# Plain passes with w2 loaded whole, factors in DRAM layout and stores moved later; first pair's w1 factors made two at a time

## The chip, the core and the metric

The kernel runs on one core of a Trainium2 chip. The metric is the device time of one execution in microseconds. A program's engines each work through their own queue in order: TensorE (PE, with its weight loads as PEld), VectorE (DVE), ScalarE (ACT), GpSimd (POOL), and SyncE (SP), which here issues all transfers.

## The reference

```python
def _attn_ref(q, k, v):                       # (8, 8, 576, 64), chunks of 64 tokens
    scores = scale * np.matmul(q_c, k_c.transpose(0, 1, 2, 4, 3))
    scores = scores - np.max(scores, axis=-1, keepdims=True)
    attn = np.exp(scores)
    attn = attn / (np.sum(attn, axis=-1, keepdims=True) + 1e-09)
    return np.matmul(attn, v_c).reshape(B, H, S, D)

def _moe_ref(x, domain_probs, w1, w2):        # x (4608, 512), 4 experts, w1 (4, 512, 1024)
    p = domain_probs / (domain_probs.sum(-1, keepdims=True) + 1e-09)
    for e in range(E):
        h = np.maximum(x @ w1[e], 0.0)
        out += p[:, e:e + 1] * (h @ w2[e])
```

Attention within chunks of 64 tokens gives x; four dense experts follow, weighted by normalized probabilities. All is in float32.

## The kernel before, in words

The 4608 tokens are 9 blocks of 512. An expert's 1024 hidden columns are two halves, so a block goes through 8 passes. Block 0 is done by the *plain passes* n = 0 to 7; the other eight blocks are four pairs, and each pair takes 8 *later passes* (8 to 39). Each float32 operand is split in a high part (fp32r, by ACT) and a low part (the rest, a subtraction), and a product is three matmuls: hi·hi, hi·lo, lo·hi.

A plain pass has eight *steps*: four hidden blocks (12 matmuls of 512 columns each, `plain_hidden`, then `relu_parts`, L614 on ACT and L615 on DVE) and four output tiles (`Tile.whole`, 12 matmuls, `Tile.out` L905 on DVE). `plain_pass` hangs work beside the steps with `add(at, i, ...)`: what is added at step i is issued behind step i on every queue. The attention of the first pair (`Beside`) is spread over the steps, ahead of each step.

A later pass uses Strassen-Winograd products: 2x2 quads of the weights and tokens, seven products instead of eight. It needs the quads' four sums s1 to s4, the *factors*, made in hi and lo parts. The first 14 products of a pass are hidden (g1..g7, h1..h7, `LaterGroup`), the 14 of the pass before are outputs (a1..a7, b1..b7, `Outer`), woven in the order of `WOVEN`; a product is 6 matmuls. The first later pass, n = 8, has the 14 hidden products alone (`FIRST`, with the last plain tile held until after its second product). The weights come as *ring units*: seven DRAM slots per pass and side (`slots`), each with two (quad or sum, group) units, loaded into three wf tiles a side (`ring_load`, `RINGS`). A unit's tile comes free when both its products are done (`ring_next`).

So the plain passes also have to make and store the factors that all later passes load:

- w2: `w_loads(1, ...)` loads four raw quads into wraw at step 6 of the pass before; `w2_split` (steps 0 and 1) makes hi and lo for the plain pass itself; `Factors` makes the sums on DVE (L389, steps 1 and 2), their parts on ACT and POOL (L343, L346) and stores them (`keep`, L411; `keep_quad`, L420) at steps 2 to 6.
- w1: passes 8 to 14 make their own, in the first pair's passes: `half_load` and `HalfFactors` load a group's columns into scratch and sum them on POOL (L444), `ring_make` makes a unit (two instructions on ACT, L488, and two on POOL, L489), uses it as ring unit and stores it (L490). `make_next` takes one from the list `making` after every product. The w1 factors of pass 7 (slots of pass 15) are made in plain passes 2 to 5 (`LAST_W1`).
- In the last plain pass `half_load`, sums and makes for pass 8 run beside the steps, then at step 6 `first_load(1)` and `probs_load`, which brings the probabilities of pass 8 that `Scaled.hidden` (L771, DVE) multiplies with.
- `Scaled.hi` and `lo` (L783 ACT, L786 POOL) split the hidden blocks of later passes; `Outer.add` (L831, L833) sums the outputs.

Of the kernel before, what the change touches and what calls it, by code (L numbers as in the profile page):

```python
# [15 lines left out]
P = 128  # L16
# [15 lines left out]
def chunk_attention_moe(ctx: ExitStack, tc: tile.TileContext, qk, v, v0, dp, w1, w2, out):  # L32
# [290 lines left out]
    def w_load(i, n, f, k):  # L323

        if i == 0 and n:
            t = opool.tile([P, 2, 2 * P], F32, name=f"acc{NK + 2 * f + k}")
        else:
            t = wpool.tile([P, 2, 2 * P], F32, name="wraw", bufs=N_RAW)
        raw[i, f, k] = t
        e, half = divmod(n % n_pass, 2)  # L330
        rows, cols = slice(2 * k, 2 * k + 2), slice(f * 2 * P, (f + 1) * 2 * P)
        nc.sync.dma_start(out=t, in_=(w1, w2)[i][e, half, :, rows, cols])

    QUADS = ((0, 0), (0, 1), (1, 0), (1, 1))

    PAIR_QUADS = ((0, 0), (1, 1), (0, 1), (1, 0))

    def w_loads(i, n, order=QUADS):
        for f, k in order:
            w_load(i, n, f, k)  # L340
# [29 lines left out]
    def w2_quad(f, k):  # L370
        return [t[:, :, f * 2 * P : (f + 1) * 2 * P] for t in w2t[k]]

    def w2_split(f, k, eng=None):
        if f == 0:
            w2t[k] = [hpool.tile([P, 2, SUB], F32R, name=f"hf{part}{4 + k}") for part in ("h", "l")]
        split(eng or nc.gpsimd, raw[1, f, k], w2_quad(f, k))

    class Factors:


        def __init__(self, i, n, quads, ws, tags):
            self.i, self.n, self.made = i, n, {}
            self.ws, self.tags = ws, dict(zip(("s1", "s2", "s3", "s4"), tags))
            for f in range(2):
                for k in range(2):
                    setattr(self, f"a{f + 1}{k + 1}", quads[f, k])

        def less(self, name, a, b, out, eng, op=ALU.subtract):
            (eng or nc.gpsimd).tensor_tensor(out=out, in0=getattr(self, a), in1=getattr(self, b), op=op)  # L389
            setattr(self, name, out)  # L390

        def sum1(self, eng=None):
            self.less("s1", "a21", "a22", self.ws[:, 0], eng, ALU.add)

        def sum2(self, eng=None):
            self.less("s2", "s1", "a11", self.ws[:, 1], eng)

        def sum3(self, eng=None):
            self.less("s3", "a11", "a21", self.a21, eng)

        def sum4(self, eng=None):
            self.less("s4", "a12", "s2", self.a12, eng)

        def make(self, name, eng=None):
            pool, tag = self.tags[name]
            t = self.made[name] = pool.tile([P, 2, *UNIT[1:]], F32R, name=tag)
            split(eng or nc.gpsimd, by_group(getattr(self, name)), parts_of(t))
# [7 lines left out]
    def keep_quad(n, f, k):  # L415

        for g in range(2):
            to = slot(n, 1, f"a{f + 1}{k + 1}", g)
            for part, t in enumerate(w2_quad(f, k)):
                nc.sync.dma_start(out=to[:, part], in_=t[:, :, g * P : (g + 1) * P].bitcast(F32))  # L420
# [7 lines left out]
    class HalfFactors:  # L428


        AT = {"a11": 0, "a12": 1, "a21": 2, "a22": 3, "s1": 4, "s2": 5, "s4": 6, "s3": 2}

        def __init__(self, n, g, places):
            self.n, self.g = n, g
            self.at = {name: places[i // 2][:, i % 2] for name, i in self.AT.items()}
            e, half = divmod(n % n_pass, 2)
            for f in range(2):
                cols = slice((2 * f + g) * P, (2 * f + g + 1) * P)
                nc.sync.dma_start(
                    out=places[f].rearrange("p a b c -> p (a b) c"), in_=w1[e, half, :, :, cols]  # L440
                )

        def less(self, name, a, b, eng, op=ALU.subtract):
            (eng or nc.gpsimd).tensor_tensor(  # L444
                out=self.at[name], in0=self.at[a], in1=self.at[b], op=op
            )

        def sum1(self, eng=None):
            self.less("s1", "a21", "a22", eng, ALU.add)

        def sum2(self, eng=None):
            self.less("s2", "s1", "a11", eng)

        def sum3(self, eng=None):
            self.less("s3", "a11", "a21", eng)

        def sum4(self, eng=None):
            self.less("s4", "a12", "s2", eng)

    halves = {}  # L460
    scratch = []

    def half_load(n, g):
        if (n, g) == (n_pass, 0):
            places = [opool.tile([P, 2, 2, P], F32, name=f"acc{NK + i}") for i in range(4)]
        else:
            if not scratch:
                scratch.append(xpool.tile([P, NK * PAIR * SUB], F32, name="xraw"))
            at = SUB + g * 7 * 2 * P
            places = [  # L470
                scratch[0][:, at + i * 4 * P : at + min(i * 4 + 4, 14) * P].rearrange(
                    "p (a b c) -> p a b c", b=2, c=P
                )
                for i in range(4)
            ]
        halves[n, g] = HalfFactors(n, g, places)
# [3 lines left out]
    n_made = (n_pass - 1) * N_SLOT  # L480
    making = []

    def ring_make(r):
        t, (n, k) = ring[0, r], divmod(r, N_SLOT)
        for u in range(2):
            g, at = divmod(2 * k + u, 7)
            src = halves[n_pass + n, g].at[ORDER[0][at]]
            nc.scalar.copy(out=t[:, u, 0], in_=src)  # L488
            nc.gpsimd.tensor_tensor(out=t[:, u, 1], in0=src, in1=t[:, u, 0].bitcast(F32), op=ALU.subtract)  # L489
        nc.sync.dma_start(out=slots[n, 0, k], in_=t.bitcast(F32))  # L490

    def make_next():
        if making:
            making.pop(0)()

    def ring_load(i, r, tag=None):

        def begin():
            ring[i, r] = wpool.tile(
                [P, 2, *UNIT[1:]], F32R, name=f"wf{RINGS[i][r % 3] if tag is None else tag}"  # L500
            )
            if i == 0 and r < n_made:
                ring_make(r)
            else:
                nc.sync.dma_start(
                    out=ring[i, r].bitcast(F32), in_=slots[r // N_SLOT % n_pass, i, r % N_SLOT]
                )

        if i == 0 and r < n_made:
            making.append(begin)  # L510
        else:
            begin()
# [110 lines left out]
    def h_alloc(s, f):  # L623
        i, k = divmod(f, 2)
        if k == 0:
            hs[s, i] = [hpool.tile([P, 2, SUB], F32R, name=f"hf{part}{2 * s + i}") for part in ("h", "l")]
        return h_part(s, f)
# [100 lines left out]
    class Scaled:  # L728
# [25 lines left out]
        def part(self, name, i):  # L754
            if (name, i) not in self.parts:
                self.parts[name, i] = hpool.tile(
                    [P, 2, SUB], F32R, name=f"hf{'hl'[i]}{self.J[name]}"
                )
            return self.parts[name, i]
# [106 lines left out]
    class Tile:  # L866
# [7 lines left out]
        def part(self, fs, cols, first, last):  # L874
# [3 lines left out]
            if self.n == 0:  # L878
# [3 lines left out]
                self.ps, parts,  # L882
                lambda f, a: h_part(self.s, f)[a][:, self.i * P : (self.i + 1) * P],
                lambda f, b: w2t[f // 2][b][:, f % 2, cols],
# [170 lines left out]
    def load_all():  # L1055
# [4 lines left out]
        w_load(0, 0, 0, 0)  # L1060
        w_load(0, 0, 1, 0)
        start_load(2, slice(0, 2))
        w_load(0, 0, 0, 1)
        w_load(0, 0, 1, 1)
        start_load(3, slice(0, 2))
        w_load(1, 0, 0, 0)
        w_load(1, 0, 1, 0)
# [7 lines left out]
    def startup(beside):  # L1075
# [36 lines left out]
        w_load(1, 0, 0, 1)  # L1112
        w_load(1, 0, 1, 1)
# [8 lines left out]
        w2_split(1, 1)  # L1122
        less_max(sc[3])
# [20 lines left out]
        w_loads(0, 1)  # L1144
        for f in range(NK):
            plain_hidden(f, [2, 3], alloc=False, name=("B1", "B0", "A0", "C0")[f])
        w2 = w2_factors(0)
        w2.sum1()
        w2.sum2()
        w2.sum3()  # L1150
        w2.sum4()
        for i, (f, k) in enumerate(QUADS):
            w1_split(f, k, (nc.gpsimd, nc.vector)[i % 2])
        for name in ("s1", "s2", "s3", "s4"):
            w2.make(name)
        for quad in KEPT:
            keep_quad(0, *quad)
        for name in ("s1", "s2", "s3", "s4"):
            w2.keep(name)
        w_loads(1, 1, PAIR_QUADS)  # L1160
# [3 lines left out]
    KEPT = ((0, 0), (0, 1), (1, 1))  # L1164

    def w2_factors(n):
        quads = {quad: raw[1, *quad] for quad in QUADS}
        ws = wpool.tile([P, 2, 2, 2 * P], F32, name="ws")
        return Factors(1, n, quads, ws, [(hpool, name) for name in ("hfh6", "hfl6", "hfh3", "hfl3")])
# [36 lines left out]
    def plain_pass(n, beside, x):  # L1206
# [5 lines left out]
        for i in range(NK):  # L1212
            add(at, i // 2, lambda i=i: w2_split(*QUADS[i]))
            if not last_pass:
                add(at, i // 2, lambda i=i: w_load(0, n + 1, *QUADS[i]))
# [3 lines left out]
        w2 = []  # L1219
        add(at, 1, lambda: w2.append(w2_factors(n)), lambda: w2[0].sum1(nc.vector), lambda: w2[0].sum2(nc.vector))  # L1220
# [396 lines left out]
```

## Time and profile before

| | us |
|---|---|
| runs of the kernel | 1532.82, 1533.34, 1535.16 (median 1533.34) |
| profiled execution | 1533.17 |
| its span, first to last instruction | 1531.4 |
| PE, DVE, POOL, ACT busy | 1477.7, 1052.6, 997.1, 630.4 |
| mean granted TensorE clock | 0.989 of full |

A row of the windows view gives a stretch's length, each engine's busy time with its instruction count, the granted clock, the share of the 16 DMA engines and GB/s. A row of the waits view reads: who waited, its line, for whom, then total us, times, longest. A row of the lines view: line, engine, operation, written tile <- read tiles, shape, count | busy us, mean ns of one | idle us before them and what ended it. A row of the timeline: start, us, engine, line, operation, tiles, count, and in brackets the idle time before it. A matmul's shown duration is longer than the distance between two starts, since matmuls overlap.

### The profile page before, as it was taken

The numbers are of one execution on the slowest core, as the hardware profiler recorded it, in microseconds if no ns is written. First come the engines' busy times: TensorE is split into PE (matmuls) and PEld (weight loads), VectorE is DVE, ScalarE is ACT, GpSimd is POOL, SyncE is SP. The second block draws the span as 40 slices with busy tenths as digits, with TensorE's granted clock in tenths as the row PEclk, the third lists the DMA queues.
The fourth block names the chain that finished last, engine by engine and source line by source line (L and its number), as shares of the span: only waits on it lengthen the run. The fifth ranks groups of instructions, "written<-read, shape, count | busy, mean of one in ns | idle before, by whom it ended". The sixth has DMA issues, their size and how long they took to land.

```text
span 1531.4 us, 23579 instructions
## 1 busy us (share of the span) xinstructions
PE 1477.7 (96%) x8556; PEld 1207.4 (79%) x8556; DVE 1052.6 (69%) x1455; ACT 630.4 (41%) x1214; POOL 997.1 (65%) x818
## 2 busy tenths in 40 slices
PE   8899977899999999999999999999999999999998
PEld 7677755677777888888888888888888888888887
DVE  5556583566767788677777886777777966666665
ACT  3456542454545443434343344334343433333332
POOL 4667677999998776555555765555557655555554
PEclk9999988999999999999999999999999999999999
DMA  7799868576767777966666579666665596565655
GB/s 222 229 294 298 296 213 269 185 263 225 251 226 247 241 244 211 269 218 215 232 207 200 201 212 268 227 213 230 203 205 195 200 234 229 195 208 194 206 193 152
DMA packets 233236, 345.13 MB, mean 225 GB/s; under 512 B 71568, under 2 KB 151200, under 8 KB 233120
## 3 DMA queue, kind: packets, MB, share of 16 engines
q1 hardware_dynamic: 233120, 343.62, 69.4%
q8 instruction: 68, 1.11, 0.3%
q14 instruction: 48, 0.39, 0.1%
HBM read 273.23 MB, written 70.33 MB: 224 GB/s over the span
## 4 chain that ended last, share of the span: by engine, by line
PE 79%; POOL 8%; DMA 4%; DVE 3%; issue 3%; ACT 2%; SPq 2%; POOLq 0%; ACTq 0%; DVEq 0%
PE A L607 43%; PE C L607 23%; PE B L607 10%; POOL hfl L786 2%; POOL wf L489 1%; DMA wraw<-in_w 1%; PE psa L208 1%; POOL xraw L444 1%; POOL hfl L346 1%; PE psa L161 1%; SPq L411 1%; POOL hfh L346 1%; DMA w<-hfh 1%; POOL wf L346 1%; DMA acc<-in_w 1%
## 5 line engine op out<-in xcount | busy, mean ns | idle before, releaser
L786 POOL TENSOR_TENSOR hfl<-wraw,hfh 128x512 fp32r<-128x512 f32 x384 | 500.7, 1319 | 229.9 <-ACT hfh L783 227.2
L607 PE MATMUL A<-xh,wf 128*128 128x512 f32 (+1 forms) x1104 | 382.1, 389 | 0.0
L607 PE MATMUL A<-hfh,wf 128*128 128x512 f32 (+1 forms) x1024 | 358.2, 391 | 0.6 <-ACT acc L831 0.6
L783 ACT CAST hfh<-wraw 128x512 fp32r<-128x512 f32 x384 | 234.2, 622 | 285.0 <-DVE wraw L777 88.8
L607 PEld LDWEIGHTS A<-xh,wf 128*128 128x128 f32 x1104 | 207.7, 189 | 43.3
L669 ACT COPY s<-A 128x512 f32<-128x512 f32 x192 | 112.8, 587 | 290.6 <-PE A L607 290.4
L607 PEld LDWEIGHTS A<-hfh,wf 128*128 128x128 f32 x1024 | 192.1, 188 | 42.9 <-DVE acc L833 1.8
L607 PE MATMUL C<-xh,wf 128*128 128x512 f32 (+1 forms) x600 | 205.9, 390 | 11.1 <-DVE acc L905 10.4
L607 PE MATMUL A<-xl,wf 128*128 128x512 f32 (+1 forms) x552 | 214.4, 389 | 0.0
L833 DVE TENSOR_TENSOR acc<-A,acc 128x512 f32<-128x512 f32 x232 | 158.0, 681 | 78.5 <-PE A L607 77.6
L607 PE MATMUL A<-hfl,wf 128*128 128x512 f32 x512 | 199.0, 389 | 0.0
L607 PE MATMUL C<-hfh,wf 128*128 128x512 f32 x512 | 178.3, 389 | 0.0
L607 PEld LDWEIGHTS C<-xh,wf 128*128 128x128 f32 x600 | 111.9, 189 | 35.1 <-DVE acc L905 10.8
L777 POOL TENSOR_TENSOR wf<-wraw,wf 128x512 f32<-128x512 f32 x31 | 40.0, 1292 | 150.3 <-DVE wf L771 150.3
L833 DVE TENSOR_TENSOR acc<-C,acc 128x512 f32<-128x512 f32 x120 | 82.7, 689 | 68.3 <-PE C L607 58.9
L607 PE MATMUL B<-xh,wf 128*128 128x512 f32 (+1 forms) x376 | 125.3, 385 | 0.0
L607 PEld LDWEIGHTS A<-xl,wf 128*128 128x128 f32 x552 | 103.9, 189 | 21.4
L786 POOL TENSOR_TENSOR hfl<-wf,hfh 128x512 fp32r<-128x512 f32 x64 | 92.8, 1451 | 40.8 <-ACT hfh L783 40.4
L607 PE MATMUL C<-xl,wf 128*128 128x512 f32 (+1 forms) x300 | 115.1, 387 | 0.0
L607 PEld LDWEIGHTS C<-hfh,wf 128*128 128x128 f32 x512 | 96.1, 188 | 19.8
L607 PEld LDWEIGHTS A<-hfl,wf 128*128 128x128 f32 x512 | 96.1, 188 | 19.5
L607 PE MATMUL C<-hfl,wf 128*128 128x512 f32 x256 | 100.2, 391 | 6.8 <-POOL hfl L786 6.8
(200 smaller groups left out, 2401.9 us busy)
## 6 DMA issues: line engine op xcount, KB each, us to landing
wf<-w SPq DMA_DIRECT2D x399, 512.0 KB, 4.2
w<-wf SPq DMA_DIRECT2D x49, 512.0 KB, 3.0
qk_in<-in_qk SPq DMA_DIRECT2D x32, 512.0 KB, 4.9
wraw<-in_w SPq DMA_DIRECT2D x36, 256.0 KB, 5.1
w<-hfh SPq DMA_DIRECT2D x32, 256.0 KB, 3.2
w<-hfl SPq DMA_DIRECT2D x32, 256.0 KB, 4.0
acc<-in_w SPq DMA_DIRECT2D x30, 256.0 KB, 5.7
xraw<-in_w SPq DMA_DIRECT2D x26, 256.0 KB, 5.0
```

The lines of the kernel that those rows point to most:

```text
L161: nc.tensor.matmul(s["sc"][of_half(half), c, slot], lhsT=q, rhs=k, start=True, stop=True)
L208: nc.tensor.matmul(av[of_half(slot % 2), half, head // 2], lhsT=s["v"][of_half(half), head], rhs=s["pt"][of_half(half), c, slot], start=Tr ...
L346: eng.tensor_tensor(out=t[1], in0=src, in1=t[0].bitcast(F32), op=ALU.subtract)
L411: nc.sync.dma_start(out=slot(self.n, self.i, name, g), in_=self.made[name][:, g].bitcast(F32))
L444: (eng or nc.gpsimd).tensor_tensor(out=self.at[name], in0=self.at[a], in1=self.at[b], op=op)
L489: nc.gpsimd.tensor_tensor(out=t[:, u, 1], in0=src, in1=t[:, u, 0].bitcast(F32), op=ALU.subtract)
L607: nc.tensor.matmul(out, lhsT=lhs(k, a), rhs=rhs(k, b), start=first and i == 0, stop=last and i == len(parts) - 1, skip_group_check=not (fi ...
L669: nc.scalar.copy(out=t, in_=self.a)
L777: (eng or nc.vector).tensor_tensor(out=self.values[place, k], in0=self.values[a, k], in1=self.values[b, k], op=op)
L783: nc.scalar.copy(out=self.part(name, 0)[:, k], in_=self.values[name, k])
L786: (eng or nc.gpsimd).tensor_tensor(out=self.part(name, 1)[:, k], in0=self.values[name, k], in1=self.part(name, 0)[:, k].bitcast(F32), op=A ...
L833: nc.vector.tensor_tensor(out=acc[key], in0=src, in1=acc[key], op=ALU.add)
```

## The change

- **w2 raw in one tile.** `w2_load` brings a pass's whole raw w2 (1 MB) in one transfer into tile hf2, at step 5 of the pass before; w1 comes as two tiles of 512 KB (wf4, wf5) at step 0 of the pass before.
- **Factors laid as in DRAM.** The tiles hfh*/hfl* become one hf tile with both parts; w2's split quads lie as [quad column group, part, block, 128], so a stored unit is contiguous. The plain pass's moving operand is then four runs of 128 columns.
- **Stores later.** The sums of w2 go to acc tiles and are made on DVE at steps 1, 3, 3, 4 (partly on POOL in passes 5 and 6); parts of s1, s2, s4, s3 at steps 4 to 7; stored as two tiles at steps 0 and 2 of the next pass. In pass 0 the sums move up.
- **First w1's factors there.** Plain passes 1 to 6 make the w1 factors of pass 0 (`FIRST_W1`) and pass 0 stores its split quads, so pass 8 loads all its ring units from DRAM. Those of pass 7 are made in plain pass 7. The w2 factors of pass 7 are made in passes 15 and 16 from raw halves and from sums kept in DRAM (`raw_load`, `keep_sums`).
- **First pair's w1 factors two at a time at fixed steps.** `make` splits a unit with one instruction each on ACT and POOL; `make_next(i)` is called at fixed places (`MAKE_AT`). The half sums go to DVE, half loads to steps 10 and 18.
- The first pair's attention ends 3 steps earlier, the token sums (`Tokens(0)`) start in pass 5; `probs_load` for pass 8 moves from step 6 to step 4.

```diff
+    def w1_load(n):
+        if n == n_pass - 1:
+            for f, k in ((0, 0), (1, 1), (1, 0), (0, 1)):
+                w1_quad_load(n, f, k)
+            return
+        for k in range(2):
+            t = wpool.tile([P, 2, HF], F32, name=f"wf{4 + k}")
+            nc.sync.dma_start(out=t, in_=of_pass(w1, n)[:, 2 * k : 2 * k + 2])
...
+    def w2_load(n, ks=(0, 1)):
+        if ks[0] == 0:
+            raw2[:] = [hf_tile(2, dtype=F32)]
...
     def w2_quad(f, k):
-        return [t[:, :, f * 2 * P : (f + 1) * 2 * P] for t in w2t[k]]
+        return [w2t[k][:, 2 * f : 2 * f + 2, part] for part in range(2)]
...
+    def make(i, r):
+
+        t, (n, k) = ring[i, r], divmod(r, N_SLOT)
+        src = staged.pop() if i else pieces(2 * k, 2)
+        nc.scalar.copy(out=t[:, :, 0], in_=src)
+        nc.gpsimd.tensor_tensor(
+            out=t[:, :, 1], in0=src, in1=t[:, :, 0].bitcast(F32), op=ALU.subtract
+        )
+        nc.sync.dma_start(out=slots[n, i, k], in_=t.bitcast(F32))
...
             product(
-                self.ps, parts,
+                self.ps.rearrange("p (a c) -> p a c", c=P), parts,
                 lambda f, a: h_part(self.s, f)[a][:, self.i * P : (self.i + 1) * P],
-                lambda f, b: w2t[f // 2][b][:, f % 2, cols],
+                lambda f, b: w2t[f // 2][:, :, b, f % 2],
...
     def plain_pass
+        add(at, 0, lambda: w2f[n - 1].keep(0))
+        add(at, 2, lambda: w2f[n - 1].keep(1))
...
+        if not last_pass:
+            add(at, 0, lambda: w1_load(n + 1))
+            for name, i, eng in zip(SUMS, (1, 2 if n == n_pass - 2 else 3, 3, 4), SUMS_ON.get(n, (v,) * 4)):
+                add(at, i, w2_do("sum", name, eng))
+            for i, quad in enumerate(KEPT):
+                add(at, 3 + i // 2, lambda quad=quad: keep_quad(n, *quad))
+            for i, (f, k) in enumerate(QUADS):
+                add(at, (3, 4, 4, 5)[i], lambda f=f, k=k: w1_split(f, k, g))
+            for name, i in zip(("s1", "s2", "s4", "s3"), (4, 5, 6, 7)):
+                add(at, i, w2_do("make", name))
+            add(at, 5, lambda: w2_load(n + 1))
...
+        for name, i in zip(SUMS, (2, 2, 3, 3)):
+            add(at, i, w2_do("sum", name, g))
+        add(at, 5, w1_make(2, "s3"), w1_make(3, "s4"))
+        for r, i in ((2, 2), (0, 3), (1, 3), (5, 5), (3, 6), (4, 6)):
+            add(at, i, lambda r=r: ring_load(0, r, (RINGS[0] + RINGS[1])[r]))
+        add(at, 4, lambda: probs_load(n + 1, 0), lambda: probs_load(n + 1, 1))
+        add(at, 6, w2_do("keep_sums"))
+        add(at, 6, lambda: first_load(1))
...
     def first_later_pass
-        add(at, 0, lambda: half_load(n + 1, 0))
-        add(at, 5, lambda: half_load(n + 1, 1))
+        add(at, 0, lambda: half_load(n + 1, 0), lambda: half_load(n + 1, 1))
...
+        half_sums(at, 0, (4, 4, 6, 6))
+        add(at, 6, lambda: make_next(0))
...
     def later_pass
+    MAKE_AT = 2, 9, 11, 14, 17, 20, 24
...
         if n + 1 < 2 * n_pass - 1:
-            add(at, 5, lambda: half_load(n + 1, 0))
-            add(at, 17, lambda: half_load(n + 1, 1))
-            half_sums(at, n + 1, 0, (9, 10, 11, 13))
-            half_sums(at, n + 1, 1, (23, 25, 26, 27))
+            add(at, 10, lambda: half_load(n + 1, 0))
+            add(at, 18, lambda: half_load(n + 1, 1))
+            half_sums(at, 0, (15, 16, 22, 22))
+            half_sums(at, 1, (22, 24))
+        if n_pass < n < 2 * n_pass - 1:
+            places = zip(SUMS, (9, 9, 10, 10)) if n == n_pass + 1 else (("s3", 9), ("s4", 10))
+            for name, i in places:
+                first.setdefault(i, []).append(lambda name=name: half_sum(1, name))
+            for i in (0, 3, *MAKE_AT[1:]) if n == n_pass + 1 else MAKE_AT:
+                first.setdefault(i, []).append(lambda: make_next(0))
+        for m, makes, raws in (
+            (2 * n_pass - 1, (22, 26), (19, 23, 27)), (2 * n_pass, (2, 8, 12, 15, 20), (4, 9, 13, 16)),
+        ):
...
-        beside = Beside(0, (n_pass - 3) * 2 * NK, True)
+        beside = Beside(0, (n_pass - 4) * 2 * NK + 5, True)
```

414 lines of the change are left out of this document (210 added, 204 removed).

## The prediction

> **What bounds the kernel now.** I read the page's head first, then the busy times pass by pass, then TensorE's (PE's) own waits, then the queues behind those waits.
>
> ```profile
> span 1531.4 us, 23579 instructions
> PE 1477.7 (96%) x8556; PEld 1207.4 (79%) x8556; DVE 1052.6 (69%) x1455; ACT 630.4 (41%) x1214; POOL 997.1 (65%) x818
> ```
>
> PE is the bound; what can be won is its idle time and the half clock that follows idle time. Both lie in the first third. By pass (start, plain passes 0 to 7, the first pair's pass 8, its passes 9 to 14, the rest):
>
> ```profile
> core 0: us, PE busy (x) PEld busy (x) DVE busy (x) ACT busy (x) POOL busy (x), PEclk, DMA share, GB/s
> 0.00:43.94 43.94, 39.93 (x464) 32.66 (x464) 25.20 (x47) 19.31 (x38) 20.94 (x22) 1.00 0.62 194
> 43.94:75.13 31.19, 25.64 (x167) 20.04 (x161) 15.08 (x25) 12.38 (x25) 17.87 (x15) 0.95 0.83 262
> 75.13:104.43 29.30, 27.02 (x228) 21.09 (x226) 14.61 (x22) 14.88 (x33) 17.96 (x14) 0.94 0.96 306
> 104.43:128.88 24.45, 24.45 (x226) 19.91 (x224) 17.88 (x27) 15.44 (x32) 17.93 (x15) 1.00 0.89 271
> 128.88:153.82 24.94, 23.57 (x165) 19.12 (x161) 14.93 (x24) 14.18 (x29) 18.67 (x16) 1.00 0.99 317
> 153.82:180.09 26.27, 24.39 (x194) 19.34 (x192) 13.80 (x21) 14.58 (x31) 18.49 (x15) 1.00 0.85 286
> 180.09:209.84 29.75, 23.95 (x97) 18.98 (x96) 20.60 (x18) 12.59 (x20) 20.92 (x14) 0.89 0.77 244
> 209.84:231.43 21.59, 18.49 (x73) 14.50 (x72) 16.85 (x15) 11.37 (x21) 16.35 (x12) 0.92 0.69 231
> 231.43:273.40 41.97, 31.46 (x125) 25.07 (x123) 16.24 (x21) 13.94 (x30) 30.64 (x35) 0.84 0.79 268
> 273.40:512.00 238.60, 224.44 (x1433) 181.44 (x1434) 157.84 (x230) 115.46 (x258) 215.44 (x218) 0.99 0.68 232
> 512.00:1531.40 1019.40, 1014.39 (x5407) 835.29 (x5405) 739.54 (x1009) 386.30 (x697) 601.92 (x452) 1.00 0.67 215
> ```
>
> From 43.94 to 512 the lengths add up to 468.06 us and PE's busy times to 423.41: **44.65 us idle**, 19.98 of it in plain passes 1 to 7, 10.51 in pass 8, 14.16 after it. Pass 3 shows what a plain pass is without a gap: 24.45 us. After 512 PE idles 5.0 us in 1019, and the change's code there is almost that of before.
>
> The clock was halved in six short stretches, each around or behind a gap (59.70:63.10, 93.90:97.30, 196.30:203.10, 227.00:230.40, 244.00:257.70, 278.20:281.60); the longest and their sum, then matmul starts in and out of such a stretch:
>
> ```profile
> 244.00:257.70 13.70, 6.16 (x15) 4.81 (x16) 1.36 (x3) 3.37 (x9) 8.51 (x12) 0.50 0.97 324
> ...
> sum 34.10, PE 22.73 PEld 17.62 DVE 16.38 ACT 8.93 POOL 27.35; mean PE 3.79 PEld 2.94 DVE 2.73 ACT 1.49 POOL 4.56
> ```
>
> ```profile
> 60.50 0.63 PE L607 MATMUL C<-hfh,hfl 128*128 128x512 f32 x1
> 60.93 0.63 PE L607 MATMUL C<-hfh,hfh 128*128 128x512 f32 x1
> 69.69 0.39 PE L607 MATMUL A<-hfh,hfh 128*128 128x512 f32 x1
> 75.13 0.39 PE L607 MATMUL B<-xh,wf 128*128 128x512 f32 x1
> ```
>
> A 512-column matmul is issued every 0.43 us there. From 69.69 to 75.13 lie two blocks of twelve: 2.72 us a block, 0.227 us a matmul. So 22.73 busy us hold 22.73 x (1 - 0.227/0.427) = **10.6 us** of lost clock. The ceiling of any repair is 44.65 + 10.6 = 55.3 us.
>
> What ends the gaps, 43.94 to 231.43 and then 231.43 to 512:
>
> ```profile
> PE C L607 <- DVE hfl L615: 7.1, 3, 4.6
> PE A L607 <- DVE hfl L615: 6.6, 4, 2.2
> PE C L607 <- ACT hfh L343: 3.3, 1, 3.3
> ...
> PE C L607 <- DVE acc L905: 10.4, 1, 10.4
> PE B L607 <- POOL hfl L786: 6.8, 3, 5.0
> PE C L607 <- POOL hfl L786: 6.8, 5, 1.4
> ```
>
> In the plain passes it is the low part of the last hidden block (L615), late on DVE; in the pair's passes DVE once, for 10.4 us, and POOL's low parts (L786).
>
> **The change part by part.**
>
> *w2 a pass ahead, stores later.* Before, the four w2 quads of the next pass are queued on SP at step 6 behind the stores of this pass's factors, and each store waits for POOL. In pass 1 ACT stands still for the quad, with the rectified block queued behind it; below it, from issue to landing by the page's part on DMA issues:
>
> ```profile
> 54.43 0.62 ACT L343 CAST hfh<-wraw 128x512 fp32r<-128x512 f32 x1 [6.82 <-DMA wraw<-in_w]
> ```
>
> ```profile
> wf<-w SPq DMA_DIRECT2D x399, 512.0 KB, 4.2
> ...
> wraw<-in_w SPq DMA_DIRECT2D x36, 256.0 KB, 5.1
> ```
>
> After, one w2 transfer goes out at step 5, into a tile (hf2) that plain passes don't use, ahead of the stores, which move to steps 0 and 2 of the next pass. From step 5 to the first split lie three 2.72 us blocks; a 256 KB quad landed in 5.1 us and 512 KB of weights in 4.2, so 1 MB lands in 6 to 8 and is hidden. What waits now: SP at step 2 for POOL's last two factors, with the following quad stores behind it, none due within a pass. In pass 0 the four sums move forward on POOL, and the next pass's w1 and w2 are loaded before the last factors are made: the 5.55 us idle of pass 1 and its stretch of half clock (3.4 x 0.47 = 1.6 us) go.
>
> *Sums moved off the due block.* Four w2 sums sit on DVE ahead of the last block's low part; they stretch when POOL works beside them:
>
> ```profile
> L389 DVE TENSOR_TENSOR ws<-ws,wraw 128x512 f32<-128x512 f32 x7 | 11.6, 1663 | 0.2
> 142.04 0.66 DVE L389 TENSOR_TENSOR wraw<-wraw 128x512 f32<-128x512 f32 x1
> ```
>
> Now one sum (0.66 to 1.66) stands ahead of it and three (2 to 5 us) behind. The gaps in passes 4 and 5 are 1.4 and 1.9 us, so they should close. The token sums start in pass 5 instead of 6 and are spread; that should take pass 6's 5.8 us and pass 7's 3.1 with it. The price is on POOL: passes 5 and 6 now have 15 of its 128x512 operations where pass 6 had 14 in 20.92 us: 15 x 1.49 = 22.4 us in a pass of 24. That is full, not over: I charge 2 us for passes 6 and 7, bounds 0 and 8.
>
> *w2 factors laid as in DRAM.* Twelve 128 KB stores a pass become six of 256 KB, and eight of 256 KB four of 512: fewer issues, same bytes. PE's moving operand becomes four runs of 128 columns instead of 512 in a row, in 48 matmuls of each plain pass. No row has such a moving operand. The lower bound is no change, the upper the half-clock step, +0.2 us each. The nearest row is ACT's write of the same layout, beside its contiguous write:
>
> ```profile
> L343 ACT CAST hfh<-wraw 128x512 fp32r<-128x512 f32 x35 | 20.8, 618 | 17.9 <-DMA wraw<-in_w 12.1 <-DMA acc<-in_w 2.8 <-DMA v_in<-in_v 2.5
> L343 ACT CAST wf<-acc 128x512 fp32r<-128x512 f32 x24 | 14.3, 621 | 0.0
> ```
>
> 618 and 621 ns: I take zero.
>
> *Pass 8.* The 10.4 us gap is DVE waiting for the probabilities, which SP issues last in step 6, behind the stores of factors and made ring units:
>
> ```profile
> DVE wraw L771 <- DMA ws<-p_t: 12.3, 1, 12.3
> ```
>
> After, they are issued at step 4. Ahead of them on SP in this pass stand two 512 KB stores, six of 256, two of 512 and three ring loads. At the 306 to 317 GB/s of passes 2 and 4 these 5 MB take 17 us; the probabilities are first used after seven blocks of 2.72 and two products of 1.36, 21.8 us. So 10.4 us go, and 6.16 x 0.47 = 2.9 of clock. Pass 8's weights now come from DRAM, so the half sums (L444) and makes (L489) that share POOL's 30.64 busy us there with the low parts leave it but for one make. They are queued ahead of b21's low part, which ends PE's 5.0 us gap at 273.3. What is late next: the half sums' loads, queued behind the store of w2's sums, and their wait is DVE's. I charge 2.5 us, bounds 0 and 13.
>
> *Passes 9 to 14.* POOL's load, 231.43 to 512:
>
> ```profile
> L786 POOL TENSOR_TENSOR hfl<-wraw,hfh 128x512 fp32r<-128x512 f32 x72 | 93.2, 1307 | 9.7 <-ACT hfh L783 9.4
> L489 POOL TENSOR_TENSOR wf<-xraw,wf 128x256 fp32r<-128x256 f32 x90 | 66.2, 757 | 11.1 <-ACT wf L488 11.0
> L444 POOL TENSOR_TENSOR xraw<-xraw 128x256 f32<-128x256 f32 x52 | 42.3, 824 | 5.6 <-DMA xraw<-in_w 5.0
> ```
>
> The half sums (42 us) go to DVE, and two makes become one of 512 columns (1.31 as L786 against 2 x 0.757, some 9 us over 45). POOL goes from 246 busy of 280.6 us to about 195, so its other gaps here (6.8 + 6.8 less the 5.0: 8.6 us) mostly close. DVE takes eight 128x256 sums a pass, at half of 0.66 to 1.66: 3 to 7 us in 39; from 158 to at most 200 of 238.6. The makes now stand at fixed steps. The tightest is at step 9, for g3 at step 12: ACT's copy of the product and its make (0.6 each, as in the rows above) and POOL's 1.31 are 2.5 us, and two products of 1.36 cover 2.72. I charge 0.7 us for each of six passes, 4.2, bounds 0 and 15.
>
> By the Trainium skill, page "SBUF — State Buffer", section "SBUF: two separate sides", DVE with two SBUF inputs and GpSimd take a port as an exclusive lock for the whole instruction. The 0.66 and 1.66 us above agree. By that rule each moved sum still stops POOL for its own third of a microsecond, some 17 us of the 42 come back to it as an estimate, and the sum would be 1494 instead of the one below.
>
> *Passes 15 and 16.* Seven w2 units are made from raw halves (1.3 us of POOL each) instead of loaded. The raw tile is single; between steps 13 and 15 a load (4 to 5 us) has 2.7 us: 1.5 us, bounds 0 and 4.
>
> *Sum.* Left over: pass 1 0.5, passes 2 to 5 2.0, 6 and 7 2.0, pass 8 2.5, 9 to 14 4.2, 15 and 16 1.5: 12.7 us. Gain 55.3 - 12.7 = 42.6. The profiled execution took 1533.17 us (span 1531.4 and 1.8 around it), 0.2 under the median of 1533.34: **1490.6 us**.
>
> A leftover gap may also cost a half-clock stretch, 3.4 x 0.47 = 1.6 us: the 2.2 us gap of pass 2 had the stretch at 93.9. The Trainium skill, page "TensorE: Matmul & The Clock Gate", section "What's actually happening", puts that at an idle window of about 3.4 us; by it such short gaps would cost only themselves, and this trace disagrees.
>
> **The rivals.**
> *Pass 8 keeps its wait.* POOL, full in passes 5 and 6, makes the last factors late; SP stands at their store with ring loads and probabilities behind it. It needs POOL 5 us late. For it: the 22.4 of 24. The gap of 10.4 + 2.9 stays: 1504.
> *The pair's passes keep their gaps.* DVE at 84% waits for half loads, or g3 waits for its make. With the 8.6 us kept and 1 us more in each of six passes: 1490.6 - 4.2 + 14.6 = 1501. For it: the 0.2 us of slack; against it, passes after 512 run gapless with DVE at 73%.
> *The plain passes become the DMA queue's.* Pass 4 has its share at 0.99 in 24.94 us. If passes 1 to 6 can't go under that: up to 1 us each, 1496.
> *Slower: the four-run operand.* 8 x 48 = 384 matmuls; above 42.6/384 = 0.11 us each it eats the gain, and at 0.2 us it costs 77: 1567. For it: no row shows such an operand. Against it: ACT's 621 ns.
> *The change doesn't do what it says*: the gaps move within the passes: within 0.2%, 1533.
>
> **How the numbers follow.** Forecast (1482 to 1499) 0.62; pass 8 0.11; pair's gaps 0.12; DMA 0.06; slower 0.06; no change 0.03. About 0.2% is what a measurement of this kernel tells from no change. Faster 0.91, same 0.03, slower 0.06. The range goes from 53 of the 55.3 us won (1480) to the pass 8 rival with 6 us of small gaps beside it (1510).
>
> **What would show it.** Right: PE's waits on L615 in the plain passes and on L786 between 231 and 512 under 2 us each, no DVE wait on p_t, passes 1 to 6 at 22 to 25 us, half clock only once or twice after 40 us. Wrong: matmul starts over 0.23 us apart in the second half of the plain passes; PE waiting for a ring unit (wf, L489's successor) at g3; DVE waiting for half loads; SP standing at a factor store when pass 8 begins.

## The result, and the profile after

| | before | after | forecast |
|---|---|---|---|
| time, median, us | 1533.51 | 1521.63 (1520.5 to 1524.5) | 1490.6 (1480 to 1510) |
| ratio to before | 1 | 0.9924, 95% interval 0.9907 to 0.9941 | 0.972 |

The change is faster, by 11.9 us (0.8%) where 42.6 were forecast. One execution of a run below (half sums later) took 3156 us and is left out of its ratio. The page of the changed kernel begins:

```profile
span 1520.5 us, 23324 instructions
...
PE 1475.2 (97%) x8556; PEld 1203.5 (79%) x8556; DVE 1081.8 (71%) x1500; ACT 626.2 (41%) x1165; POOL 964.6 (63%) x720
```

The same matmuls run in both kernels, so the place of the loss is found by cutting both traces at the same products. The cuts are the first product of pass 1, the first of pass 8, and three score products of the second pair's attention, in the middle of pass 9, at the end of pass 13 and in the middle of pass 17. So the stages are passes 1 to 7; pass 8 and half of 9; the rest of 9 to 13; and 14 to half of 17. In the windows view of the kernel before they are:

```profile
43.94:234.16 190.22, 170.25 (x1149) 135.24 (x1143) 114.50 (x151) 95.42 (x191) 130.92 (x98) 0.96 0.85 273
234.16:296.40 62.24, 46.20 (x182) 36.56 (x180) 25.68 (x32) 21.54 (x46) 50.10 (x54) 0.86 0.67 224
296.40:482.61 186.21, 179.00 (x1187) 145.08 (x1188) 127.49 (x189) 94.31 (x211) 167.04 (x170) 1.00 0.73 246
482.61:623.83 141.22, 139.80 (x684) 114.48 (x675) 110.53 (x144) 56.34 (x103) 101.14 (x81) 1.00 0.72 229
```

and in the changed kernel, with two stretches for later use (the products that the prediction counts as pass 8 to pass 14, and pass 6):

```profile
44.23:219.03 174.80, 164.29 (x1147) 133.50 (x1143) 114.57 (x150) 93.65 (x185) 129.95 (x91) 0.98 0.78 277
219.03:272.86 53.83, 44.82 (x182) 35.12 (x180) 27.23 (x37) 17.62 (x31) 33.12 (x26) 0.94 0.68 236
272.86:461.30 188.44, 180.54 (x1187) 144.78 (x1188) 149.31 (x224) 91.24 (x178) 141.03 (x105) 1.00 0.72 243
461.30:612.30 151.00, 142.69 (x687) 113.81 (x677) 118.48 (x152) 60.58 (x106) 109.84 (x79) 1.00 0.73 232
...
216.31:490.70 274.39, 256.47 (x1559) 204.74 (x1558) 203.60 (x300) 123.39 (x238) 199.29 (x149) 0.99 0.71 241
...
174.50:196.26 21.76, 21.76 (x97) 18.01 (x96) 15.78 (x15) 11.98 (x20) 21.76 (x13) 1.00 0.70 247
```

So the first two stages gain 15.4 and 8.4 us, and the next two lose 2.2 and 9.8 again; 0.3 us are lost ahead of the first cut and 0.6 behind the last. Of the 9.8 us, 9.7 lie in passes 15 and 16: they take 39.4 and 46.8 us where they took 38.3 and 38.2. What PE waits for in these stages now, in the same order (the waits view):

```profile
PE psa L208 <- ACT pt L198: 6.4, 4, 2.7
PE A L638 <- POOL hf L364: 3.1, 2, 1.8
PE A L638 <- DVE hf L646: 1.0, 1, 1.0
...
PE A L638 <- DMA wf<-w: 5.4, 1, 5.4
PE A L638 <- ACT s L701: 2.3, 1, 2.3
...
PE C L638 <- DVE B L836: 2.9, 3, 1.4
...
PE A L638 <- DVE acc L863: 3.3, 5, 1.7
PE A L638 <- POOL hf L816: 1.6, 1, 1.6
```

The waits of before are nearly gone: DVE's low part in the plain passes is down to a single 1.0 us, the 10.4 us wait in pass 8 is not there, and POOL's low parts (now L816) hold PE up nowhere between 219 and 461. Those listed are new, and behind most of them another engine waits. On ACT:

```profile
55.45 0.60 ACT L645 ACTIVATE hf<-B 128x512 fp32r<-128x512 f32 x1 [2.06 <-PE B L638]
55.95 0.58 ACT L194 COPY pt<-psa 128x512 f32<-128x512 f32 x1
56.56 1.49 ACT L198 COPY pt<-psa 32x256 f32<-32x256 f32 x4
...
556.42 0.62 ACT L501 CAST wf<-v_in 128x512 fp32r<-128x512 f32 x1 [5.51 <-DMA v_in<-w_sums]
556.95 0.61 ACT L813 CAST hf<-wraw 128x512 fp32r<-128x512 f32 x1
...
570.90 0.62 ACT L501 CAST wf<-v_in 128x512 fp32r<-128x512 f32 x1 [5.53 <-DMA v_in<-w_sums]
...
577.65 0.62 ACT L501 CAST wf<-v_in 128x512 fp32r<-128x512 f32 x1 [5.65 <-DMA v_in<-w_sums]
```

In pass 1 ACT places the probabilities of the attention only behind the last hidden block's rectifier, and PE's next work is the product that reads them. In pass 16 ACT stands three times for the raw form of a w2 unit (each time for sums that pass 7 kept in DRAM, `w_sums`), with the hidden casts queued behind. DVE stands at half sums (L489) for their load:

```profile
234.68 1.96 DVE L489 TENSOR_TENSOR xraw<-xraw 128x256 f32<-128x256 f32 x2 [3.82 <-DMA xraw<-in_w]
...
292.74 1.09 DVE L489 TENSOR_TENSOR xraw<-xraw 128x256 f32<-128x256 f32 x1 [3.03 <-DMA xraw<-in_w]
293.75 0.69 DVE L836 TENSOR_TENSOR B<-C,s 128x512 f32<-128x512 f32 x1
```

and SP's own rows show what is ahead of the half loads and of the ring unit that PE then misses for 5.4 us (the first of the three at 239.69):

```profile
221.46 2.86 SPq L468 DMA_DIRECT2D w_sums<-acc  x4
...
225.34 5.50 SPq L484 DMA_DIRECT2D xraw<-in_w  x4
230.89 3.59 SPq L424 DMA_DIRECT2D w<-hf  x4
234.57 0.56 SPq L536 DMA_DIRECT2D wf<-w  x1
...
235.92 2.85 SPq L424 DMA_DIRECT2D w<-hf  x4
...
239.69 2.43 SPq L536 DMA_DIRECT2D wf<-w  x3
```

### The profile page after: what moved, and what is told of

Its sections match the earlier page's. It is cut to its first block, busy times and chain, and to the rows that moved or that the text cites. A ratio compares the mean times of both kernels' runs of the same rounds, so it can differ in the third digit from the quotient of the medians.

```text
span 1520.5 us, 23324 instructions
## 1 busy us (share of the span) xinstructions
PE 1475.2 (97%) x8556; PEld 1203.5 (79%) x8556; DVE 1081.8 (71%) x1500; ACT 626.2 (41%) x1165; POOL 964.6 (63%) x720
## 4 chain that ended last, share of the span: by engine, by line
PE 61%; DMA 1%; DVE 0%; ACT 0%; POOL 0%; SPq 0%; issue 0%; DVEq 0%; ACTq 0%
PE A L638 34%; PE C L638 17%; PE B L638 8%; PE psa L208 1%; PE psa L161 1%; DMA out<-pt 0%; DMA v_in<-w_sums 0%; DVE acc L863 0%; DVE wraw L807 0%; ACT pt L198 0%; POOL wf L502 0%; POOL hf L816 0%; DVE pt L971 0%; PE C L1596 0%; PE psa L638 0%
## 5 line engine op out<-in xcount | busy, mean ns | idle before, releaser
L816 POOL TENSOR_TENSOR hf<-wraw,hf 128x512 fp32r<-128x512 f32 x384 | 506.6, 1334 | 247.3 <-ACT hf L813 245.0
L638 PE MATMUL A<-hf,wf 128*128 128x512 f32 x1536 | 394.5, 392 | 14.1 <-DMA wf<-w 5.4
L813 ACT CAST hf<-wraw 128x512 fp32r<-128x512 f32 x384 | 234.7, 622 | 303.8 <-DVE wraw L807 99.5
L638 PEld LDWEIGHTS A<-hf,wf 128*128 128x128 f32 x1536 | 286.4, 188 | 80.8 <-DVE acc L863 11.1
L638 PE MATMUL C<-hf,wf 128*128 128x512 f32 x768 | 195.1, 389 | 1.0 <-POOL wf L502 0.6
L638 PEld LDWEIGHTS C<-hf,wf 128*128 128x128 f32 x768 | 144.0, 188 | 31.6 <-POOL wf L502 1.1
L816 POOL TENSOR_TENSOR hf<-wf,hf 128x512 fp32r<-128x512 f32 x64 | 91.9, 1436 | 33.7 <-ACT hf L813 33.3
L807 DVE TENSOR_TENSOR wraw<-wf,wraw 128x512 f32<-128x512 f32 x64 | 92.7, 1448 | 10.2 <-POOL hf L816 9.0
L638 PE MATMUL B<-hf,wf 128*128 128x512 f32 x384 | 97.7, 389 | 0.8 <-POOL hf L816 0.8
L807 POOL TENSOR_TENSOR wraw<-wraw 128x512 f32<-128x512 f32 x64 | 91.9, 1437 | 0.0
```

Of the source, the lines that this page charges most:

```text
L638: nc.tensor.matmul(out, lhsT=lhs(k, a), rhs=rhs(k, b), start=first and i == 0, stop=last and i == len(parts) - 1, skip_group_check=not (fi ...
L807: (eng or nc.vector).tensor_tensor(out=self.values[place, k], in0=self.values[a, k], in1=self.values[b, k], op=op)
L813: nc.scalar.copy(out=self.part(name, 0)[:, k], in_=self.values[name, k])
L816: (eng or nc.gpsimd).tensor_tensor(out=self.part(name, 1)[:, k], in0=self.values[name, k], in1=self.part(name, 0)[:, k].bitcast(F32), op=A ...
```

## The experiments

My theory after this reading: the change does what it says, and at four places, each with its own cause, new waits hold most of the 31 us that are missing. The rival: the engines and the transfers are simply full there, and a wait taken away comes back at the next product. The first edits below take them one at a time. Stage lengths of every run, read at the same products (unchanged stages differ by some 3 us from trace to trace; the last four runs follow further down):

| us | passes 1 to 7 | 8 to mid 9 | mid 9 to 13 | 14 to mid 17 | ratio to before (95%) |
|---|---|---|---|---|---|
| before | 190.2 | 62.2 | 186.2 | 141.2 | 1 |
| after | 174.8 | 53.8 | 188.4 | 151.0 | 0.9924 (0.9907 to 0.9941) |
| two raw tiles | 174.9 | 53.9 | 189.6 | **145.5** | 0.9880 (0.9866 to 0.9895) |
| w2's sums stored later | 177.9 | **49.9** | 189.7 | 152.0 | 0.9907 (0.9892 to 0.9922) |
| spare step | **167.3** | 53.3 | 186.4 | 153.5 | 0.9868 (0.9853 to 0.9882) |
| half sums later | 176.3 | 52.6 | **181.6** | 150.4 | 0.9880 (0.9860 to 0.9899) |
| all those stores later | 174.7 | **46.4** | 188.2 | 152.6 | 0.9889 (0.9871 to 0.9906) |
| sums on DVE | **171.4** | **56.5** | 186.4 | 153.2 | 0.9911 (0.9897 to 0.9924) |
| five edits | 163.9 | 47.2 | 180.8 | 143.4 | 0.9714 (0.9700 to 0.9727) |
| before, early probabilities | 191.4 | 60.0 | 186.3 | 141.2 | 0.9978 (0.9968 to 0.9988) |
| five edits, half sums back on POOL | 164.0 | **54.4** | **186.9** | 145.5 | 0.9797 (0.9781 to 0.9812) |
| five edits, sums back ahead | **166.9** | 47.0 | 181.0 | 143.4 | 0.9723 (0.9707 to 0.9740) |
| five edits, load back behind the stores | **206.8** | 46.4 | 181.5 | 142.8 | 0.9982 (0.9973 to 0.9990) |

**Two raw tiles** for the w2 units of passes 15 and 16, each load issued a make earlier:

```diff
-        src = staged.pop() if i else pieces(2 * k, 2)
+        src = staged.pop(0) if i else pieces(2 * k, 2)
-        k, t = unstaged.pop(0), load.tile([P, 2, 2, P], F32, name="v_in")
+        k = unstaged.pop(0)
+        t = (load, att)[k % 2].tile([P, 2, 2, P], F32, name=("v_in", "pt")[k % 2])
-            (2 * n_pass - 1, (22, 26), (19, 23, 27)), (2 * n_pass, (2, 8, 12, 15, 20), (4, 9, 13, 16)),
+            (2 * n_pass - 1, (22, 26), (19, 21, 23, 27)), (2 * n_pass, (2, 8, 12, 15, 20), (4, 9, 13)),
```

> Starting from the changed kernel (1521.6 us). In passes 15 and 16 the seven w2 units are made from raw halves that pass through one tile, and ACT stands 5.5 to 5.7 us at each of three loads of it, with hidden casts and product copies queued behind. Theory (the single tile): with two tiles, each loaded one make earlier, ACT's stands there fall to under 1 us, PE's excess between 540 and 595 us falls from about 10 us to 2 or less, and the time is 1512 to 1514. Rival (the makes' own work on ACT and POOL, 0.62 + 1.3 us each, is what costs): the gaps stay, 1520 to 1522.

The stage goes from 151.0 to 145.5 us and ACT's long stands are gone, but 1516.82 us is above the 1512 to 1514 expected. The theory holds for over half of the stage's 9.8 us, and for 7.4 of the 9.7 in passes 15 and 16 themselves, which now take 39.4 us each. Some 4 us are left in the stage; the longest waits of PE among them are for DVE's sums of products at the start of pass 14 (1.0) and for POOL's low part in pass 16 (0.8). Whether the makes' own work causes them isn't shown.

**w2's sums stored later**:

```diff
@@ plain_pass (pass 7)
-        add(at, 6, w2_do("keep_sums"))
@@ first_later_pass (pass 8)
+        add(at, 9, lambda: w2f[n - 1].keep_sums())
```

> Starting from the changed kernel (1521.6 us). The four stores of w2's sums (1 MB) move from step 6 of pass 7 to behind step 9 of pass 8, so the half loads and the first w2 ring units of the pair are issued ahead of them on SP. Theory (SP's queue was filled with stores): DVE's 3.8 us wait for the half loads and PE's 2.29 us gap at 236.9 go, PE's 5.41 us gap for a ring unit at 240.8 falls to 1 to 3 us, 4 to 9 us in all with the half clock behind it: 1513 to 1518. Rival (the stores of w1's last factors, 2 MB ahead of the same ring unit, set that gap): the 2.29 goes and the 5.41 stays, 1519 to 1520. Second rival (DMA bandwidth, the same bytes in the same stretch): under 1 us, 1521.

PE's longest wait in this run's pass 8:

```profile
PE A L638 <- DMA wf<-w: 4.7, 1, 4.7
```

1519.69 us, the first rival: the 2.3 us gap goes, the ring unit's stays at 4.7. **All those stores later** has, instead of that edit in pass 8, w1's last factors moved too:

```diff
-        for name in ("s1", "s2"):
-            add(at, 0, lambda name=name: last_w1[0].keep(name))
-        for name in ("s3", "s4"):
-            add(at, 2, lambda name=name: last_w1[0].keep(name))
+        for name in ("s3", "s4"):
+            add(at, 9, lambda name=name: last_w1[0].keep(name))
+        for name in ("s1", "s2"):
+            add(at, 10, lambda name=name: last_w1[0].keep(name))
+        add(at, 11, lambda: w2f[n - 1].keep_sums())
```

> Starting from the changed kernel (0.9924 of before, 1521.6 us). All 3 MB of stores that stand on SP between the end of pass 7 and the pair's first w2 ring unit are issued behind that unit: w1's last factors (2 MB) from steps 0 and 2 of pass 8 to steps 9 and 10, w2's sums (1 MB) to step 11. Theory (the stores ahead of it on SP delay the ring unit, 2.8 us for each MB as the run with w2's sums alone moved showed): PE's gaps of 2.29 and 5.41 us at 236.9 and 240.8 both go, and the half clock behind them: 7 to 9 us, 1513 to 1515. Rival (ACT stands at the t3 product of pass 9 for the late store of the tile hf6, or the following ring units queue behind the stores): 3 to 6 us of the gain come back as a gap 5 to 10 us later, 1517 to 1520.

PE's two longest waits in pass 8 now:

```profile
PE B L638 <- POOL hf L816: 1.8, 1, 1.8
PE A L638 <- DMA wf<-w: 1.1, 1, 1.1
```

Pass 8's stage falls by 7.4 us, with no half clock left in it. The stores ahead on SP were the cause of both gaps. Between runs this edit's gain of the whole time is 5.4 us of 1534.9 (0.9924 less 0.9889), and 1517.96 us lies in the rival's range: a new wait of 1.8 us for POOL stands in pass 8, and the last stage is 1.6 us longer, which is within the spread of unchanged stages.

**Spare step**: where two attention stages share a step.

```diff
-            self.rate, self.due = (5 * PAIR * NT + 1) / n, 0.5
+            self.rate, self.due = (5 * PAIR * NT + 1) / n, 0.45
```

> Starting from the changed kernel (1521.6 us). One number: the attention's due count begins at 0.45 instead of 0.5. Its 41 stages now share 37 steps, so at four steps two stages are issued together; with 0.5 two of these pairs are the empty stage and the product with the values, which leaves no block between ACT's placing (L194, L198) and PE's product. With 0.45 all four pairs are the product and the next maximum. Theory (the lost spare step): the gaps of 2.68 us in pass 1 and 2.27 us in pass 2 go, the 1.0 beside the latter and the half clock from 87.8 to 94.7 with them: 5 to 9 us, 1513 to 1517. Rival (ACT and DVE are simply late there, whatever the step): the gaps move to the next block, 1520 to 1522.

What is left of the placing among PE's waits in passes 1 to 7:

```profile
PE psa L208 <- ACT pt L198: 1.4, 2, 0.8
```

Of the 6.4 us for the placing 1.4 stay, and the half clock of pass 2 is gone: 7.5 us, and 1514.41 in all. The theory holds.

**Half sums later**:

```diff
-            half_sums(at, 1, (22, 24))
+            half_sums(at, 1, (26, 27))
```

> Starting from the changed kernel (1521.6 us). The first two sums of the second half, on DVE, move from steps 22 and 24 to 26 and 27; their load is still issued at step 18. Theory (DVE stands at the sum for its load, 3.0, 0.8 and 1.5 us in three passes, with the pass's sums of products behind it): PE's gaps for DVE B L836 and the acc behind it in passes 9 to 13 (1.53 + 0.92, 0.32 + 1.15, 1.56 + 0.76) go: 4 to 6 us, 1516 to 1518. Rival (DVE's added work itself, 0.4 to 1.5 us a sum, is what is late): gaps of the same size at later products, 1520 to 1522.

Passes 9 to 13 lose 6.8 us and no PE wait for DVE's B L836 is left. The theory holds, a little above its range of 4 to 6 us.

**Sums on DVE**, three of pass 6:

```diff
-        n_pass - 2: (nc.vector, nc.gpsimd, nc.gpsimd, nc.gpsimd),
+        n_pass - 2: (nc.vector, nc.vector, nc.vector, nc.vector),
```

> Starting from the changed kernel (0.9924 of before, 1521.6 us). In pass 6 three of the four w2 sums go from POOL to DVE, so POOL has 12 operations instead of 15. Theory (POOL is full from 171 to 222 us, and its backlog makes w2's low parts late in pass 7): PE's gaps of 1.35 and 1.80 us at 207.5 and 210.5 go, 1518 to 1519. Rival (DVE's sums stand ahead of the rectified blocks' low parts, and run POOL at 2.3 instead of 1.3 us an operation): PE waits for L646 in pass 6 by 1 to 3 us, no gain: 1521 to 1523.

PE's two longest waits from pass 7 to the cut in pass 9:

```profile
PE A L638 <- DMA wf<-w: 4.4, 1, 4.4
PE A L638 <- ACT s L701: 2.9, 1, 2.9
```

Neither was quite right: both gaps go and the plain passes get 3.4 us shorter, as the theory said, and pass 8's stage gets 2.7 us longer. PE idles only 0.5 us more there (9.0 to 9.6), but the wait for ACT grows from 2.3 to 2.9 us, and a half-clock stretch more (237.65 to 241.07) begins at its end. The ratio can't be told from the change's own.

**Five edits**: two raw tiles, spare step, half sums later, all those stores later, sums on DVE.

> The changed kernel with five edits together: two raw tiles, the attention's count from 0.45, the half sums at steps 26 and 27, the stores of w1's last factors and w2's sums behind the first w2 ring units, three sums of pass 6 on DVE. Theory (five separate places, gains add): 5.5 + 8 + 5 + 8 + 3 = 29 us less than the changed kernel's 1521.6, 1491 to 1496. Rival (a gap closed at one place comes back at the next, since POOL, SP and the DMA queue are full there): half of it, 1503 to 1508.

The page of this run:

```profile
span 1487.6 us, 23325 instructions
...
PE 1466.6 (99%) x8556; PEld 1199.9 (81%) x8556; DVE 1088.9 (73%) x1503; ACT 625.9 (42%) x1165; POOL 960.9 (65%) x717
```

1490.75 us (1489.35 to 1491.8), the best of all versions. The gains add: by the ratios the five alone gain 0.0192 in all, and together 0.0210. POOL's relief in pass 6 now counts: the plain passes are 3.4 us shorter than with the spare step alone, and pass 8 gives at most 0.8 of it back (47.2 against 46.4).

**The kernel before with the early probabilities alone**:

```diff
-        add(at, 6, lambda: first_load(1), lambda: probs_load(n + 1, 0), lambda: probs_load(n + 1, 1))
+        add(at, 4, lambda: probs_load(n + 1, 0), lambda: probs_load(n + 1, 1))
+        add(at, 6, lambda: first_load(1))
```

> The kernel before, with one part of the change alone: the two loads of the probabilities for pass 8 are issued at step 4 of pass 7 instead of last in step 6. Theory (the step of the prediction: this place on SP is what DVE waits for): the 10.42 us gap at 241 goes with 2.9 us of half clock, 1520 to 1524 against 1534. Rival (the next thing is late at once: the half sums and makes on POOL, or a ring unit): 3 to 8 us of it come back as gaps for POOL's low parts or a ring unit within 20 us, 1525 to 1531.

PE's waits in pass 8, where the kernel before had the 10.4 and a 5.0:

```profile
PE A L607 <- ACT s L669: 6.8, 2, 4.8
PE B L607 <- POOL hfl L786: 3.5, 1, 3.5
PE C L607 <- DVE acc L905: 1.8, 1, 1.8
```

1531.53 against 1534.95, ratio 0.9978 (0.9968 to 0.9988). The rival, a little beyond its range: the one wait of 10.4 us falls to 1.8, POOL's 5.0 to 3.5, and ACT is late instead, by 6.8; it had itself stood 9.5 us for a half load. So the early probabilities alone are worth little; the rest of what pass 8 gains came with the change's other parts.

The last three undo one part of the change each, on top of the five edits, where no other wait hides what comes back. **Half sums back on POOL**:

```diff
@@ half_sum
-        (eng or nc.vector).tensor_tensor(out=to, in0=a, in1=b, op=op)
+        (eng or nc.gpsimd).tensor_tensor(out=to, in0=a, in1=b, op=op)
```

> The version with the five edits (0.9714 of before, 1490.8 us), where a wait that comes back is not hidden by others; here the 48 half sums of the pair's passes go back from DVE to POOL (0.74 us each as before the change, 36 us). Theory (the move is what closed POOL's 8.6 us of gaps in passes 9 to 14): PE's waits for POOL's low parts come back, 5 to 9 us, 1496 to 1500. Rival (making two units with one operation, 1.3 us against 2 x 0.76, was enough): under 2 us, 1490 to 1493.

PE's two longest waits in passes 8 to 13:

```profile
PE A L639 <- DMA wf<-w: 6.8, 1, 6.8
PE B L639 <- POOL hf L817: 3.4, 3, 1.5
```

1503.88, ratio 0.9797 (0.9781 to 0.9812): 13 us dearer. POOL's gaps come back (3.9 us of PE's time in passes 9 to 13, which are 6.1 us longer), and 7.2 us come in pass 8, which I had not expected: PE waits there for a ring unit again. SP stands 8.0 us at the store of a made unit, whose low part POOL makes behind the half sums, and the ring unit's load is queued behind that store.

**Sums back ahead**:

```diff
-            for name, i, eng in zip(SUMS, (1, 2 if n == n_pass - 2 else 3, 3, 4), SUMS_ON.get(n, (v,) * 4)):
+            for name, i, eng in zip(SUMS, (1, 1, 2, 2), SUMS_ON.get(n, (v,) * 4)):
```

> The version with the five edits (1490.8 us); the four w2 sums of a plain pass go back to steps 1, 1, 2 and 2, ahead of the last two rectified blocks' low parts on DVE. Theory (these sums made the low part L615 of before late): PE's waits for DVE at the fifth block come back at 1 to 2 us in four or five passes, with a half-clock stretch or two: 5 to 10 us, 1496 to 1501. Rival (the load of the raw w2, now a pass ahead, was what delayed the chain): under 2 us, 1490 to 1493.

PE's longest wait in the plain passes:

```profile
PE A L639 <- DVE hf L647: 2.3, 1, 2.3
```

1492.03, ratio 0.9723 (0.9707 to 0.9740), not to be told from 0.9714: the rival. Passes 1 to 7 are 3 us longer in the trace, no more than unchanged stages differ.

**Load back behind the stores**:

```diff
-        add(at, 0, lambda: w2f[n - 1].keep(0))
-        add(at, 2, lambda: w2f[n - 1].keep(1))
+        if n == 1:
+            add(at, 0, lambda: w2f[0].keep(0))
+            add(at, 2, lambda: w2f[0].keep(1))
...
-            add(at, 5, lambda: w2_load(n + 1))
+            add(at, 6, lambda: w2f[n].keep(0))
+            add(at, 7, lambda: w2f[n].keep(1), lambda: w2_load(n + 1))
```

> The version with the five edits (1490.8 us); the stores of w2's sums' factors go back from steps 0 and 2 of the next pass to steps 6 and 7 of their own, with the load of the next w2 behind them. Theory (SP stands at a store for POOL's last factors, the load of w2 goes out 2 to 6 us later, ACT stands for it with the rectified blocks behind): PE gaps at the fifth block of passes 2 to 7, 5 to 15 us in all, 1496 to 1506. Rival (a load of 5.5 us has five blocks to land in): under 2 us, 1490 to 1493.

ACT's waits in the plain passes are headed by:

```profile
ACT hf L361 <- DMA hf<-in_w: 36.8, 4, 10.1
```

1532.29, ratio 0.9982 (0.9973 to 0.9990): 41 us dearer, far beyond my range. Passes 1 to 7 take 206.8 us. With the raw w2 in one transfer a late load stops all four splits, and the attention's placing queued behind them on ACT: PE waits for that 14.5 us. These 41 us are not what the move of the load was worth in the change: before, four quads of 256 KB were loaded at step 6, and passes 1 to 7 took 190.2 us.

## Why the prediction was right or wrong

- **The step that failed**: the 12.7 us left over in the sum. It put at nothing the attention's placing in the plain passes (7.5 us, spare step) and the stores ahead of the first w2 ring unit (most of the 7.4 us, all those stores later). It had DVE's stands at the half loads only as a rival (6.8 us, half sums later), and charged 1.5 us for the raw loads of passes 15 and 16, where they cost 9.7 and two tiles take back 7.4.
- **Direction, and the ceiling**: right. The five edits reach 1490.75 with the clock granted in full, so 44 of the 55.3 us can be won (1534.95 less 1490.75). That this is the forecast's own number is chance, since five further edits were needed for it.
- **Passes 1 to 7**: the working leaves 4.5 us of 26.1 (19.98 idle, and 6.1 of clock, the 10.6 less pass 8's 2.9 and 1.6 of the stretch at 278.2), a gain of 21.6; it is 15.4. The load of w2 ahead of the stores matters, as put (41 us with the one large transfer; its share of the 15.4 isn't shown). The sums moved off the due block, to which the working gave the gaps of passes 4 and 5, show little: with them back ahead the trace is 3 us longer and the time can't be told apart. The moved token sums were not tried alone. What failed is what I left out: the last hunk of the diff, which gives the attention 37 steps instead of 40. The way its stages fall on these steps costs 7.5 us, and passes 1 and 2 take 26.0 and 30.9 us where the sign of being right was 22 to 25. POOL in passes 6 and 7, charged at 2, cost 3.1. There the price of one operation was too low: 1.49 us was the mean of before, and pass 6 now holds 13 operations in 21.76 us, 1.67 each.
- **Pass 8**: the 10.4 us went, and the half loads behind the store of w2's sums came next, as named: 2.3 us of PE, for 2.5 charged. But the same queue also held the first w2 ring unit, 5.4 us and a half-clock stretch; I had checked only the probabilities against it. (The rows that the working calls pass 7, pass 8 and passes 9 to 14 end three quarters into pass 7, in pass 9 and in pass 14; its sums don't suffer from that.)
- **Passes 9 to 14**: POOL's busy time is 199 us of 274, for 195 forecast, and its gaps closed, by the move of the half sums at least in part (3.9 us of PE come back without it, of 8.6; two makes in one were not tried alone); g3 never waits for its unit, so the 0.7 us a pass was charged for the wrong thing. What took the place is the rival's mechanism, DVE at the half loads: 9.1 us of DVE in four waits, 3.8 of them in pass 8. I had priced the moved sums (30.4 us in all, 48 of 648 ns, inside my 3 to 7 a pass) but not what they wait for. From 21.6 follows a forecast gain of 22.5 for passes 8 to 14 (42.6 and the 1.5 charged to passes 15 and 16, less 21.6); measured are 8.4 - 2.2 = 6.2.
- **Passes 15 and 16**: right mechanism, wrong size: 1.5 (at most 4) charged, 9.7 measured. I priced one load against one short interval. Each of the later loads stands behind the store of the unit made just before, which waits for POOL, and then takes 3.5 to 5.5 us to land; ACT stood 17.6 us in four waits and everything behind it with it. The cause of the 2.3 us that are left with two tiles is open.
- **Four-run operand**: the cost of nothing is right, and the slower rival falls with it. Twenty-four matmuls of pass 1's second half, all with that operand, take 5.44 us, 0.227 each, as with the contiguous one:

```profile
64.82 0.39 PE L638 MATMUL A<-hf,hf 128*128 128x512 f32 x1
...
70.26 0.39 PE L638 MATMUL B<-xh,wf 128*128 128x512 f32 x1
```

- **The port**: by the Trainium skill, page "SBUF — State Buffer", section "SBUF: two separate sides", whichever of DVE (two SBUF inputs) and GpSimd starts first holds the shared port for its whole instruction. The 17 us that I estimated from it for the moved sums did not show: POOL is 4 us above the forecast that left it out. The working doesn't say how 17 us of POOL make 1494. The moved sums themselves took 0.42 us in the median and 0.65 in the mean.
- **The rivals as alternatives**: they came in part and together. I gave a chance to each alone, and the forecast charged each leftover as if the others were settled.

## What to carry to other kernels

Ask of every transfer that a change moves or adds what stands ahead of it on its queue, and of every work that moves to another engine what it waits for and what stands behind it there: three of the four losses were in-order engines standing for a late load. A gap that is closed ahead of a late transfer can come back behind it, as a wait or as a half-clock stretch (sums on DVE: 3.4 us gained, 2.7 given back), though it need not (spare step: 7.5 gained, nothing given back in pass 8); so try such an edit again when the later wait is closed. Read the small hunks of a diff too: one rate in a scheduler cost as much as a queue.

## What the runs showed of the hardware

In these traces the half clock is decided on a fixed grid. In the kernel before its stretches start at 59.7, 93.9, 196.3, 227.0, 244.0 and 278.2 us: the later ones 10, 40, 49, 54 and 64 times 3.413 us behind the first. What counts is less a gap's length than the idle share of one grid window. The 2.68 us gap of pass 1 in the changed kernel lies in two windows (PE idle 1.66 and 1.02) and costs no clock; two shorter ones in pass 2 leave 2.12 of 3.41 us idle in one window, and 6.8 us at half clock follow:

```profile
53.67:57.08 3.41, 1.75 (x8) 1.13 (x6) 2.27 (x5) 1.58 (x4) 0.68 (x1) 1.00 1.01 407
57.08:60.49 3.41, 2.39 (x69) 2.13 (x70) 0.89 (x2) 2.69 (x8) 1.29 (x1) 1.00 0.62 233
84.39:87.80 3.41, 1.29 (x5) 0.52 (x3) 3.34 (x7) 1.21 (x4) 1.28 (x1) 1.00 0.47 179
87.80:94.63 6.83, 5.68 (x73) 4.79 (x74) 1.38 (x3) 3.38 (x8) 3.74 (x3) 0.50 0.30 88
```

All 38 stretches between 40 us and the last 6 us of a trace, in the twelve traces that have one (the five edits together have none), follow a grid window with at least 1.79 us of PE idle; of the windows with more than that, two kept the clock, with 1.82 (before, early probabilities) and 1.91 (load back behind the stores). The Trainium skill, page "TensorE: Matmul & The Clock Gate", section "What's actually happening", has the free-running window of 3413 ns, which agrees; that it takes a whole idle window does not.
